# A gated mix of a state-space convolution and a bilinear GLU: first weights, four sums, ScalarE groups, last tile, dummy matmuls and plan numbers changed together

## The chip, the cores and the metric

The kernel runs on one core of a Trainium2 chip. The metric is the time of one execution on the device in microseconds (us), and lower is better. The core has a matrix engine (TensorE, PE in the profile, with its weight loads shown apart as PEld), VectorE (DVE), ScalarE (ACT), GpSimd (POOL) and SyncE (SP). Each engine takes its instructions in the order in which they were issued to it, and engines wait for one another by semaphores. Matmuls write to PSUM, of which the kernel uses eight banks of 128 partitions x 512 fp32 numbers (two for `y`, one each for `pg` and `pu`, four for everything else, `ps_k`). Transfers (DMAs) are issued from queues of SyncE, ScalarE and GpSimd.

## The reference

The input `x` has 2048 rows of 512 channels. Two branches work on it, and a gate for each row mixes them:

```python
x = A_u
g = _sigmoid((x * gate_w).sum(-1, keepdims=True))
a = _A_ref(x, ...)   # long convolution by FFT, with a kernel K made from 128 states per channel
b = _B_ref(x, B_w_gate, B_w_up, B_w_down)   # ((x Wg) * (x Wu)) Wd, with 1792 hidden columns
return g * a + (1 - g) * b
```

In branch a, `K = 2 Re sum_n C_n exp(A_n dt l)` for 2048 positions l and 512 channels; then `y = irfft(rfft(u) * rfft(K))` and `+ u * D_skip`. All numbers are fp32.

## The kernel before

**The GLU (branch b).** The 2048 rows are four tiles of 512 (`ci`), the 1792 hidden columns 14 blocks of 128 (`f`) in five groups (`GROUPS`). A hidden step, `hidden(f)`, multiplies a block of gate weights (`pg`) and of up weights (`pu`) with the tokens of a tile. There are 56 steps. Each fp32 operand is split into a high part, rounded to the matmul's own format, and the low rest (`split`: ScalarE copies the high part, VectorE subtracts), and three matmuls (`THREE`) replace one. The two products are multiplied into `h`, which is split into `hh` and `hl` by ScalarE and VectorE. `down` then multiplies the split `h` by the down weights into a sum `y` for each 128 rows (`r` = 0 to 3), over all blocks of the group. There are two PSUM banks for `y`.

**The sums.** `evacuate` scales a finished `y` by `ngate` = 1 - g of its rows (ScalarE, into one of three `acc` buffers) and stores it: the first time for a row tile by a plain store from SyncE, later by an accumulating transfer from GpSimd. The last tile of the last group goes another way, `ends`: what has been accumulated is read back into `sums` (in the profile `kt`), `product_in` adds the gated `y`, `transform_in` adds the convolution's last quarter, and `store` writes each 128 rows.

**The gate.** `u_part(c)` for c = 0 to 7 loads rows of `u`, makes the gate's scores with VectorE and the first transform with TensorE. After every second part, ScalarE and VectorE make `gate` and `ngate` for one tile of 512 rows.

**The convolution (branch a).** VectorE and ScalarE make tables of powers: `amplitudes` (21 exponentials for two blocks of channels, in three groups of seven), `phases` (sines) and the products. TensorE turns them into K and transforms K and u (`k_block`, `k_first`, `m_second`, `m_inverse`, `m_last`, all in the PSUM tag `k`). `finish` multiplies the result by the gate: eight ScalarE activations as one piece of work, except in the last quarter, where VectorE does it.

**The order of work.** Nothing runs in the order in which the code states it. Each `add(engine, us, fn, r=..., w=..., rank=...)` hands a piece of work to a planner (`Work`). The planner simulates all engines with the stated durations, takes the piece that can start first (ties by `rank`, lower first) and so writes out one fixed order for each engine. It knows buffer counts, a DMA rate (`DMA_RATE`), how far SyncE may issue ahead of the transfers (`AHEAD`), and the times at which TensorE's instruction code is fetched (`CODE...`; `recs` counts the instructions of a piece). Hidden step n may not be planned before `T_STEP * (n - 1)`. On the chip the engines keep the planned order but wait on semaphores, not on the planned times.

**The start.** `first_loads` loads tokens of tile 0 in four pieces (`x01`, `x23`; in the profile `y<-in_xT`) and the first two blocks of gate and up weights in eight pieces (`w01`; in the profile `ev<-in_wts`). Two of the eight go out on ScalarE's queue, both of block 1, and six on SyncE's. A piece is 128 partitions of two rows of 512 bytes. `split_block` splits a piece: ScalarE rounds (`whi`), VectorE subtracts (`wlo`). Meanwhile TensorE runs two dummy fp32 matmuls of 512 columns on a zeroed tile (`warm`); the profile shows each as two passes (`k<-acc`). `first_products` then takes blocks 0 and 1 together, in the order of the pieces.

Of the kernel before, what the change touches and what calls it, by code (L numbers as in the profile page):

```python
# [115 lines left out]
T_STEP = 10.1  # L116
# [30 lines left out]
class Work:  # L147
# [15 lines left out]
    CODE_US, CODE_BUS, PACE = 3.5, 0.9, 0.114  # L163
    DMA_RATE = 0.32
    AHEAD = 4.0
# [146 lines left out]
def gated_mix_kernel(  # L312
# [3 lines left out]
    xT: bass.AP,  # L316
    wts: bass.AP,
# [86 lines left out]
    def split(hi, lo, s, key):  # L404
# [9 lines left out]
        add("act", 0.62, lambda: act.copy(high(), src()), r=[got], w=[ph], rank=0)  # L414
# [19 lines left out]
    def first_loads():  # L434
# [9 lines left out]
        def first_w(f, kt):  # L444
            return w01.t[:, 2 * f : 2 * f + 2].rearrange("p c (k d) -> p c k d", k=KT)[:, :, kt]
# [159 lines left out]
    def down(y, r, h, w, first, last):  # L605
        def fn():
            for n, (a, b) in enumerate(THREE):
                pe.matmul(
                    y.t, h[a].t[:, r * P : (r + 1) * P], w[b].t, start=first and n == 0, stop=last and n == 2
                )  # L610

        add("pe", 0.684, fn, r=[*h, *w], w=[y], rank=2, recs=6)
# [3 lines left out]
    def evacuate(gi, ci, r, y):  # L616
# [4 lines left out]
        acc = new("glu", "acc", [P, D], bufs=3)  # L621
        add(
# [13 lines left out]
    def ends():  # L636
# [7 lines left out]
        def product_in(r, y):  # L644
            t = t0 + r
            add(
                "dve", 0.69,
                lambda: dve.scalar_tensor_tensor(
                    sums.t[:, r], y.t, ngate[:, t : t + 1], sums.t[:, r], op0=ALU.mult, op1=ALU.add
                ),  # L650
                r=[y, (m_gate, LAST)], w=[(sums, r)], rank=0,
# [12 lines left out]
        def store(r):  # L664
            add(
# [839 lines left out]
```

## Time and profile before

| what | us |
|---|---|
| median of 3 runs (602.71 to 603.29) | 602.87 |
| the profiled execution | 601.65 |
| its span, first to last instruction | 599.9 |
| ScalarE busy in it | 407.1 |
| sixteen matmul groups of K (`k<-v,x`) busy | 33.4 |
| matmuls of the GLU's last product (`y<-dhi,hl`), busy | 90.6 |

The profiled execution is one run of the program by itself, so its span and its time are compared with each other first and with the median afterwards. Rows of the views give the start (in order of time), the length, the engine, the operation and the tiles as output<-inputs; in brackets stands how long the engine had been idle before and what ended that. All rows name line L102, the helper that issues every instruction, so the tiles tell them apart.

### The profile page before, as it was taken

To read this page: it belongs to the slowest core of one execution; us is meant where nothing else is said; L and a number is where in the kernel's file an instruction comes from. 1 tells how busy PE (TensorE), PEld (TensorE's weight loads), DVE (VectorE), ACT (ScalarE), POOL (GpSimd) and SP (SyncE) were. 2 spreads that over 40 slices of the span, in tenths; PEclk is the share of its full clock that TensorE was granted. 3 is DMA by queue.
4 is the path that set the end of the run, shared out by engine and by line. 5 is a ranking of instruction groups with operands and counts; after the bars stand their busy time and mean duration, and the time that the engine had idled before them with its cause. 6 is when DMAs were issued, how large, how long until landed. Compare 5 with 4: busy or idle time off the path is not lost.

```text
span 599.9 us, 16215 instructions
## 1 busy us (share of the span) xinstructions
PE 590.1 (98%) x6628; PEld 452.7 (75%) x6628; DVE 513.7 (86%) x813; ACT 407.1 (68%) x923; POOL 106.4 (18%) x165
## 2 busy tenths in 40 slices
PE   8999999999999999999999999999999999999997
PEld 5667777777778877787877778787777777778875
DVE  6968999999999999999999998999999444874343
ACT  5658878875897887759789767869865545452330
POOL 0343443331212102010121101011110101211110
PEclk9999999999999999999999999999999999999999
DMA  8799968659859789399999849997994899997655
GB/s 264 221 343 343 317 211 285 205 147 277 210 121 291 206 238 320 65 306 211 301 228 254 224 125 274 215 302 156 309 233 156 209 212 297 253 239 164 158 83 112
DMA packets 102223, 136.22 MB, mean 227 GB/s; under 512 B 7300, under 2 KB 68228, under 8 KB 101124
## 3 DMA queue, kind: packets, MB, share of 16 engines
q1 hardware_dynamic: 80788, 100.57, 54.6%
q0 software_dynamic: 20672, 34.35, 28.6%
q8 instruction: 52, 0.85, 0.6%
q10 hardware_dynamic: 688, 0.26, 0.2%
q14 instruction: 23, 0.19, 0.1%
HBM read 77.75 MB, written 57.41 MB: 225 GB/s over the span
## 4 chain that ended last, share of the span: by engine, by line
PE 88%; DVE 7%; DMA 3%; issue 1%; ACT 1%; SPq 0%; DVEq 0%; POOLq 0%
PE pg L102 23%; PE pu L102 23%; PE y L102 22%; PE k L102 18%; DVE v L102 2%; DVE x L102 2%; DMA x_d<-x 1%; DMA s_d<-ts 1%; DMA ev<-in_wts 1%; DVE m L102 1%; DVE h L102 1%; DVE t L102 1%; DVE hl L102 1%; DVE ri L102 0%; DVE y L102 0%
## 5 line engine op out<-in xcount | busy, mean ns | idle before, releaser
L102 PE MATMUL pg<-x,whi 128*128 128x512 f32 x440 | 136.6, 390 | 0.8 <-ACT whi L102 0.8
L102 PE MATMUL pu<-x,whi 128*128 128x512 f32 x440 | 136.6, 390 | 0.0
L102 POOL DMA_DIRECT2D out<-acc x52 | 44.7, 924 | 304.9 <-ACT acc L102 293.7
L102 PEld LDWEIGHTS pg<-x,whi 128*128 128x128 f32 x440 | 82.6, 188 | 19.1 <-ACT whi L102 2.4
L102 PEld LDWEIGHTS pu<-x,whi 128*128 128x128 f32 x440 | 82.6, 188 | 16.9
L102 PE MATMUL y<-dhi,hl 128*128 128x512 f32 x224 | 90.6, 404 | 2.1 <-DVE hl L102 1.6
L102 PE MATMUL pg<-x,wlo 128*128 128x512 f32 x220 | 88.3, 402 | 0.1
L102 PE MATMUL pu<-x,wlo 128*128 128x512 f32 x220 | 88.0, 400 | 0.0
L102 PE MATMUL y<-dlo,hh 128*128 128x512 f32 x224 | 87.6, 391 | 0.0
L102 PE MATMUL y<-dhi,hh 128*128 128x512 f32 x224 | 87.3, 390 | 0.0
L102 ACT CAST hh<-h 128x512 fp32r<-128x512 f32 x56 | 34.8, 621 | 48.2 <-DVE h L102 47.6
L102 ACT ACTIVATE acc<-y,ngate 128x512 f32<-128x512 f32 x68 | 45.7, 687 | 27.2 <-PE y L102 18.4
L102 DVE TENSOR_TENSOR h<-pu,h 128x512 f32<-128x512 f32 x55 | 37.7, 685 | 27.6 <-PE pu L102 27.3
L102 PEld LDWEIGHTS y<-dhi,hl 128*128 128x128 f32 x224 | 42.0, 187 | 20.6 <-issue 4.8
L102 ACT COPY ts<-k 128x512 f32<-128x512 f32 (+1 forms) x112 | 47.7, 500 | 14.3 <-PE k L102 14.2
L102 PEld LDWEIGHTS pu<-x,wlo 128*128 128x128 f32 x220 | 41.3, 188 | 17.3 <-issue 8.2
L102 PEld LDWEIGHTS pg<-x,wlo 128*128 128x128 f32 x220 | 41.3, 188 | 15.5 <-issue 5.2
L102 PEld LDWEIGHTS y<-dhi,hh 128*128 128x128 f32 x224 | 42.1, 188 | 9.2
L102 PEld LDWEIGHTS y<-dlo,hh 128*128 128x128 f32 x224 | 42.1, 188 | 7.8
L102 ACT COPY h<-pg 128x512 f32<-128x512 f32 x55 | 32.2, 586 | 22.5 <-PE pg L102 14.5
L102 POOL DMA_DIRECT2D s_d<-ts x64 | 39.6, 626 | 40.7 <-ACT ts L102 36.3
L102 DVE TENSOR_TENSOR hl<-h,hh 128x512 fp32r<-128x512 f32 x56 | 38.4, 685 | 6.7 <-ACT hh L102 6.6
(117 smaller groups left out, 1006.3 us busy)
## 6 DMA issues: line engine op xcount, KB each, us to landing
x<-x_d SPq DMA_DIRECT2D x32, 512.0 KB, 6.2
out<-acc POOLq DMA_DIRECT2D x52, 256.0 KB, 6.7
in<-s_d SPq DMA_DIRECT2D x24, 512.0 KB, 6.0
raw<-in_wts SPq DMA_DIRECT2D x36, 256.0 KB, 4.6
x_d<-x POOLq DMA_DIRECT2D x16, 512.0 KB, 6.8
s_d<-ts POOLq DMA_DIRECT2D x64, 128.0 KB, 5.6
y_d<-ts SPq DMA_DIRECT2D x16, 512.0 KB, 5.6
raw<-in_xT SPq DMA_DIRECT2D x28, 256.0 KB, 5.0
```

What stands on the lines that cost most here:

```text
L102: got = getattr(self.engine, name)(*args, **kw)
```

## The change

- The first weights come from an input of their own, `in_w01`, laid out by the four row blocks `kt`: 128 partitions of 2 KB, of which block 0 is the first half. ScalarE's queue now loads `kt` = 0 for block 0 and then for block 1; SyncE loads both blocks of `kt` = 1 to 3 in one transfer each. The high part of the very first piece of tokens is copied by VectorE.
- The dummy matmuls are five of 256 columns.
- The sums of tile 0 in the first group are copied to `acc` first and gated there in place.
- The exponentials go in seven groups of three; the gating in `finish` goes in groups of two.
- In `ends`, `transform_in` goes ahead of `product_in`, and the last 128 rows are multiplied, added and stored in two halves of 256 columns.
- `T_STEP`, `CODE_US`, `CODE_BUS`, `DMA_RATE` and `AHEAD` have other values.

```diff
-T_STEP = 10.1
+T_STEP = 10.01
...
-    CODE_US, CODE_BUS, PACE = 3.5, 0.9, 0.114
-    DMA_RATE = 0.32
-    AHEAD = 4.0
+    CODE_US, CODE_BUS, PACE = 4.6, 1.0, 0.114
+    DMA_RATE = 0.327
+    AHEAD = 3.3
...
-        add("act", 0.62, lambda: act.copy(high(), src()), r=[got], w=[ph], rank=0)
+        if key == ("x", 0, 0):
+            add("dve", 0.4, lambda: dve.tensor_copy(high(), src()), r=[got], w=[ph], rank=0)
+        else:
+            add("act", 0.62, lambda: act.copy(high(), src()), r=[got], w=[ph], rank=0)
...
         def first_w(f, kt):
-            return w01.t[:, 2 * f : 2 * f + 2].rearrange("p c (k d) -> p c k d", k=KT)[:, :, kt]
+            return w01.t[:, kt].rearrange("p (f c d) -> p f c d", f=2, c=2)[:, f]
...
-        def first_block(f, kt, engine="sp"):
-            rows_w = wts[f][:, : 2 * D].rearrange("p (c k d) -> k p c d", c=2, k=KT)[kt]
-            queue = act if engine == "act" else sp
-            add(engine, 0.42, lambda: queue.dma_start(first_w(f, kt), rows_w), w=[(w01, (f, kt))], dma=128, rank=-1)
-
-        first_block(1, 0, "act")
-        first_block(1, 1, "act")
+        def first_block(kt, f=None):
+            fs = range(2) if f is None else [f]
+            queue = sp if f is None else act
+            cs = slice(2 * P * fs[0], 2 * P * fs[-1] + 2 * P)
+            add(
+                "sp" if f is None else "act", 0.42, lambda: queue.dma_start(w01.t[:, kt, cs], w01s[kt][:, cs]),
+                w=[(w01, (f, kt)) for f in fs], dma=128 * len(fs), rank=-1,
+            )
+
+        first_block(0, 0)
+        first_block(0, 1)
         for kt in range(KT):
             first_x(kt)
-            first_block(0, kt)
-            if kt > 1:
-                first_block(1, kt)
+            if kt:
+                first_block(kt)
...
-        add("dve", 0.2, lambda: dve.memset(zero.t, 0.0), w=[zero], rank=-1)
+        add("dve", 0.2, lambda: dve.memset(zero.t[:, :256], 0.0), w=[zero], rank=-1)
...
-            for _ in range(2):
-                pe.matmul(scratch.t, zero.t[:, :P], zero.t, start=True, stop=True)
-
-        add("pe", 3.4, warm, r=[zero], w=[scratch], rank=-1, recs=8)
+            for _ in range(5):
+                pe.matmul(scratch.t[:, :256], zero.t[:, :P], zero.t[:, :256], start=True, stop=True)
+
+        add("pe", 4.3, warm, r=[zero], w=[scratch], rank=-1, recs=20)
...
-    def down(y, r, h, w, first, last):
+    def down(y, r, h, w, first, last, half=None):
+        cs = slice(0, D) if half is None else slice(half * D // 2, half * D // 2 + D // 2)
...
         acc = new("glu", "acc", [P, D], bufs=3)
+        if gi == 0 and ci == 0:
+            add("act", 0.59, lambda y=y: act.copy(acc.t, y.t), r=[y], w=[acc], rank=0)
+            y = acc
         add(
             "act", 0.69, lambda: act.activation(acc.t, y.t, AF.Copy, scale=ngate[:, t : t + 1]),
...
-        def product_in(r, y):
+        def product_in(r, y, half=None):
             t = t0 + r
+            cs = slice(0, D) if half is None else slice(half * D // 2, half * D // 2 + D // 2)
             add(
-                "dve", 0.69,
+                "dve", 0.69 if half is None else 0.42,
...
+            add(
+                "sp", 0.42, lambda: sp.dma_start(ov[:, t, cs], sums.t[:, r, cs]), r=[(sums, (r, half))], w=[(m_out, (t, half))],
+                dma=256 if half is None else 128, rank=-1,
             )
...
         for r, y in ending[:2]:
+            transform_in(r)
             product_in(r, y)
-            transform_in(r)
-            store(r)
         for r, y in ending[2:]:
             transform_in(r)
-        for r, y in ending[2:]:
-            product_in(r, y)
-            store(r)
+        product_in(*ending[2])
+        for half in range(2):
+            product_in(*ending[3], half)
...
-                        if f not in late:
+                        if gi + 1 == len(GROUPS) and ci == LAST and r == 3 and f == fs[-1]:
+                            for half in range(2):
+                                down(ys[r], r, hs[f], wd[f], False, half == 1, half)
+                        elif f not in late:
...
-        for n in range(3):
-            ks = range(7 * n, 7 * n + 7)
-            add("act", 0.17 + 1.29 * (n == 0) + 7 * (0.09 + 0.0009 * TB * len(bs)), lambda ks=ks: exps(ks), r=[par], w=[(e, n)])
+        for n in range(7):
+            ks = range(3 * n, 3 * n + 3)
+            add("act", 0.1 + 1.29 * (n == 0) + 3 * (0.09 + 0.0009 * TB * len(bs)), lambda ks=ks: exps(ks), r=[par], w=[(e, n)])
...
-            add("act", 3.0, gated, r=ga, w=[fin])
+            for j in range(2 * n):
+                ts = range(2 * j, 2 * j + 2)
+                add("act", 0.7, lambda ts=ts, gated=gated: gated(ts), r=[*ga, (fin, 0), (fin, 1)], w=[(fin, ("g", j))])
```

More of the change, by code (lines that the diff above doesn't have):

```diff
@@ L316, in gated_mix_kernel @@
     xT: bass.AP,
+    w01s: bass.AP,
     wts: bass.AP,
@@ L608, in fn @@
                 pe.matmul(
-                    y.t, h[a].t[:, r * P : (r + 1) * P], w[b].t, start=first and n == 0, stop=last and n == 2
+                    y.t[:, cs], h[a].t[:, r * P : (r + 1) * P], w[b].t[:, cs], start=first and n == 0, stop=last and n == 2
                 )
-        add("pe", 0.684, fn, r=[*h, *w], w=[y], rank=2, recs=6)
+        add("pe", 0.684 if half is None else 0.37, fn, r=[*h, *w], w=[y if half is None else (y, half)], rank=2, recs=6)
     ending, stored = [], set()
@@ L643, in ends @@
         )
-        def product_in(r, y):
+        def product_in(r, y, half=None):
             t = t0 + r
+            cs = slice(0, D) if half is None else slice(half * D // 2, half * D // 2 + D // 2)
             add(
-                "dve", 0.69,
+                "dve", 0.69 if half is None else 0.42,
                 lambda: dve.scalar_tensor_tensor(
-                    sums.t[:, r], y.t, ngate[:, t : t + 1], sums.t[:, r], op0=ALU.mult, op1=ALU.add
+                    sums.t[:, r, cs], y.t[:, cs], ngate[:, t : t + 1], sums.t[:, r, cs], op0=ALU.mult, op1=ALU.add
                 ),
-                r=[y, (m_gate, LAST)], w=[(sums, r)], rank=0,
+                r=[y if half is None else (y, half), (m_gate, LAST), (sums, r)], w=[(sums, (r, half))], rank=0,
+            )
+            add(
+                "sp", 0.42, lambda: sp.dma_start(ov[:, t, cs], sums.t[:, r, cs]), r=[(sums, (r, half))], w=[(m_out, (t, half))],
+                dma=256 if half is None else 128, rank=-1,
             )
@@ L662, in transform_in @@
             )
-        def store(r):
-            add(
-                "sp", 0.42, lambda: sp.dma_start(ov[:, t0 + r, :], sums.t[:, r]), r=[(sums, r)], w=[(m_out, t0 + r)],
-                dma=256, rank=-1,
-            )
         for r, y in ending[:2]:
+            transform_in(r)
             product_in(r, y)
-            transform_in(r)
-            store(r)
         for r, y in ending[2:]:
             transform_in(r)
-        for r, y in ending[2:]:
-            product_in(r, y)
-            store(r)
+        product_in(*ending[2])
+        for half in range(2):
+            product_in(*ending[3], half)
     def glu():
@@ L1366, in finish, with gated @@
                 continue
-            def gated(t0=t0, flat=flat):
-                for t in range(4 * n):
+            def gated(ts, t0=t0, flat=flat):
+                for t in ts:
                     act.activation(flat()[:, t], flat()[:, t], AF.Copy, scale=gate[:, t0 + t : t0 + t + 1])
-            add("act", 3.0, gated, r=ga, w=[fin])
+            for j in range(2 * n):
+                ts = range(2 * j, 2 * j + 2)
+                add("act", 0.7, lambda ts=ts, gated=gated: gated(ts), r=[*ga, (fin, 0), (fin, 1)], w=[(fin, ("g", j))])
         cs = slice(P * q, P * q + P)
@@ L1475 @@
         "in_xT": host(u[rows.T.reshape(L)].T),
+        "in_w01": host(
+            np.stack([by_tile(i["B_w_gate"])[:2], by_tile(i["B_w_up"])[:2]], axis=1)
+            .reshape(2, 2, P, KT, P)
+            .transpose(3, 2, 0, 1, 4)
+            .reshape(KT, P, 4 * P)
+        ),
         "in_wts": host(
```

## The prediction, made before the changed kernel ran

> **What bounds the kernel now.** I read the page first, then the waits of TensorE, then the busy time by stages, and last the order of time at three places that the change touches.
>
> ```profile
> span 599.9 us, 16215 instructions
> PE 590.1 (98%) x6628; PEld 452.7 (75%) x6628; DVE 513.7 (86%) x813; ACT 407.1 (68%) x923; POOL 106.4 (18%) x165
> ```
>
> TensorE (PE) is busy for 590.1 of 599.9 us. The matmuls are the same before and after, except for some dummy ones and the last output tile. So the change can win only what TensorE does not use: 9.8 us in all. The waits of TensorE say where these lie:
>
> ```profile
> PE y L102 <- DVE hl L102: 1.6, 3, 0.7
> PE k L102 <- DVE acc L102: 1.5, 1, 1.5
> PE pg L102 <- ACT whi L102: 0.8, 1, 0.8
> PE k L102 <- DVE in L102: 0.6, 1, 0.6
> PE y L102 <- ACT acc L102: 0.4, 1, 0.4
> PE k L102 <- issue: 0.2, 1, 0.2
> PE k L102 <- DVE y L102: 0.2, 1, 0.2
> PE y L102 <- DVE kt L102: 0.2, 1, 0.2
> ```
>
> They add up to 5.5 us. The other 4.3 us are the end, after the last matmul (tail, below). By stages (the columns are length, then the busy time of PE, PEld, DVE, ACT and POOL, the granted clock, the DMA share and GB/s):
>
> ```profile
> 30.00:45.00 15.00, 13.74 (x67) 9.33 (x66) 10.05 (x20) 8.41 (x28) 7.16 (x12) 1.00 1.00 342
> 240.00:440.00 200.00, 200.00 (x2873) 154.39 (x2871) 196.89 (x287) 159.46 (x383) 24.07 (x25) 1.00 0.89 227
> ```
>
> From 30 to 45 us TensorE idles for 1.26 us, while the DMA engines are full. From 240 to 440 us it never idles, and the granted clock is 1.00: nothing is to be had there. VectorE (DVE) is nearly full there as well (196.89 of 200), which matters for a rival below.
>
> **The head.** The first real matmul needs three things: the end of the dummy matmuls, the first piece of tokens (tile `x`), and the first rounded piece of weights (`whi`).
>
> ```profile
> 0.73 0.98 ACTq L102 DMA_DIRECT2D ev<-in_wts  x2
> 0.92 0.48 DVE L102 MEMSET acc<- 128x512 f32 x1 [0.92 <-PEq L1494]
> 1.46 3.78 PE L102 MATMUL k<-acc 128*128 128x512 f32 x4 [1.46 <-DVE acc L102]
> 4.71 0.62 ACT L102 CAST x<-y 128x512 fp32r<-128x512 f32 x1 [1.16 <-DMA y<-in_xT]
> 5.57 1.02 ACT L102 CAST whi<-ev 128x256 fp32r<-128x256 f32 x3 [0.24 <-DMA ev<-in_wts]
> 6.03 0.50 PE L102 MATMUL pg<-x,whi 128*128 128x512 f32 x1 [0.79 <-ACT whi L102]
> ev<-in_wts ACTq DMA_DIRECT2D x2, 128.0 KB, 4.6
> L102 DVE TENSOR_SCALAR x<-v 128x512 f32<-128x512 f32 x1 | 0.4, 427 | 0.0
> ```
>
> Tokens are there at 4.71, and ScalarE (ACT) rounds them for 0.62 us. The weights that SyncE sent second are there only at 5.57. Rounding them brings the first matmul at 6.03, 0.46 us after their landing. After the change the block that is needed first leaves ScalarE's queue first, at 0.73; with the 4.6 us of that queue it lands at about 5.3 (estimate), and the first matmul could start at 5.3 + 0.46 = 5.8. The tokens no longer stand in its way: VectorE takes their high part, at the 0.43 us of the nearest one-source row, and is done by 4.71 + 0.43 = 5.14. The low part follows on VectorE's own queue, 0.2 us sooner than behind ScalarE's copy. The dummy matmuls: 4 passes over 512 columns took 3.78 us, 0.9 each, so 10 passes over 256 columns take about 4.3 to 4.7. The memset is half as wide (0.24 instead of 0.48), so they start at 1.22 and end at 5.5 to 5.9. They last about as long as the data takes. I take 5.7, a little under the 5.8 because the rows of the new block are twice as long: a gain of **0.3 us**. Three of SyncE's issues fall away (three double blocks instead of six), so its later loads only come sooner. Bounds: 0.7 (landing at 4.7 like the tokens, dummies sped up) and a loss of 0.1 (second block late; it is wanted two matmuls after the first).
>
> [...]
>
> **The four ungated sums.** These rows are TensorE's, ScalarE's and VectorE's in order of time:
>
> ```profile
> 30.77 0.39 PE L102 MATMUL y<-dhi,hh 128*128 128x512 f32 x1
> 34.07 1.09 PE L102 MATMUL k<-y,w_t 32*64 32x512 f32 x8 [0.19 <-DVE y L102]
> 34.56 0.21 ACT L102 ACTIVATE gate<-gate 128x4 f32<-128x4 f32 x1 [5.09 <-DVE y L102]
> 35.79 1.09 PE L102 MATMUL k<-in,w_t 32*64 32x512 f32 x8 [0.64 <-DVE in L102]
> 36.53 1.26 ACT L102 ACTIVATE acc<-y,ngate 128x512 f32<-128x512 f32 x2
> 37.26 0.50 PE L102 MATMUL y<-dhi,hl 128*128 128x512 f32 x1 [0.38 <-ACT acc L102]
> 38.01 0.62 ACT L102 CAST x<-raw 128x512 fp32r<-128x512 f32 x1 [0.23 <-DMA raw<-in_xT]
> 38.66 0.69 DVE L102 TENSOR_TENSOR x<-raw,x 128x512 fp32r<-128x512 f32 x1 [0.48 <-ACT x L102]
> 41.47 0.39 PE L102 MATMUL pg<-x,wlo 128*128 128x512 f32 x1
> L102 ACT COPY h<-pg 128x512 f32<-128x512 f32 x55 | 32.2, 586 | 22.5 <-PE pg L102 14.5 <-DVE hl L102 6.2 <-DVE ev L102 1.3
> ```
>
> The first two sums of tile 0 are complete at 31.2 (30.77 + 0.39); they fill both `y` banks and sit there until the gate exists, at 36.5. In the meantime TensorE has only the first transform of `u`, whose inputs VectorE is still making. It waits 0.19 + 0.64 + 0.38 = 1.21 us. With a plain copy (0.59, the nearest row of the same shape) ScalarE empties both banks by 31.2 + 2 x 0.59 = 32.4, in the 5.09 us in which it now waits for the gate, so the four copies (4 x 0.59 = 2.4 us) are covered: the first two wholly, the others where ScalarE has 6.6 of 15 us free (row 30 to 45). Then the 18 matmuls that now start at 37.26 (4.2 us to 41.47) can fill the hole. What is late next is the last quarter of the next tokens: rounded from 38.01, its low part is done by 38.66 + 0.69 = 39.35, and TensorE wants it at 41.47 - 1.21 - 0.3 = 39.96. That leaves 0.6 us. I take **1.0 us**, with bounds 0 (tokens as late as the gain) and 1.6 (the two halves of the transform also run without the drain between them). The fourth sum finds no free `acc` buffer (three, and the gate must come first) and keeps its bank as now.
>
> **ScalarE's groups in pieces.** The gated groups of eight now go in twos, and the exponentials in threes instead of sevens. No instruction is added; other work of ScalarE can now step in between.
>
> ```profile
> 2.26 1.28 ACT L102 ACT_TABLE_LOAD   x1 [2.26 <-issue]
> ```
>
> Every wait of TensorE is in the list above, and besides the gate's only the three for `hl` can hang on ScalarE, 1.6 us together. I take 0 of them, with bounds 0 and 1.6; the second rival has them all. If a sine steps in between two pieces of exponentials, ScalarE loads its tables twice more, 2.6 us. That costs TensorE nothing as long as it has other work, which it had throughout from 240 to 440 us; without that cover it is another wait for `hl`, and counted with the third rival.
>
> **The plan's numbers.** `T_STEP`, `CODE_US`, `CODE_BUS`, `DMA_RATE` and `AHEAD` only change the order in which the planner puts work, on every engine and queue. 0.09 us less per hidden step is 5 us at the last of 56. The code fetches they plan for show in one wait of TensorE, 0.2 us, that I count as gone: **0.2 us**. The rest I take as 0, between -1 and +1: these are the `hl` waits that can go or come.
>
> **The tail.**
>
> ```profile
> 595.00 0.19 PEld L102 LDWEIGHTS y<-dhi,hh 128*128 128x128 f32 x1
> 595.22 0.39 PE L102 MATMUL y<-dhi,hh 128*128 128x512 f32 x1
> 595.65 0.75 DVE L102 SCALAR_TENSOR_TENSOR kt<-y,ngate,kt 128x512 f32<-128x512 f32 x1 [1.29 <-PE y L102]
> 596.43 0.33 SPq L102 DMA_DIRECT2D out<-kt  x1
> L102 DVE SCALAR_TENSOR_TENSOR v<-v 128x256 f32<-128x256 f32 x16 | 6.7, 419 | 0.0
> DMA to landing us min/median/max: 2.0/2.0/2.3
> ```
>
> From the last matmul's end (595.61) to the span's end pass 4.3 us: VectorE 0.75, the store 2.3 from its issue, and 1.2 for the ending. Afterwards three matmuls become six of half width. The 18 matmuls above took 4.21 us, 0.234 each; half of it is 0.117, but each brings a weight load of 0.19. I take 0.19, between 0.117 and 0.234. The last of six starts at 594.76 + 5 x 0.19 = 595.71 and ends 0.27 later, at 595.98 instead of 595.61. VectorE starts 0.04 after it, as now, and needs 0.48: 0.75 less 0.27, the difference between 0.69 (512 columns, above) and 0.42 (256). The store leaves at 596.53, 0.10 later than now; the one of the first half has left SyncE's queue by then (0.33 each). It carries 128 KB instead of 256; at the 342 GB/s of the stage above that is 0.38 less. The sum is a gain of **0.25 us**: at best 0.5 (0.117 per matmul), at worst a loss of 0.3 (0.234, and a landing of 2.3 whatever the size).
>
> [...]
>
> The order of the last sums changes too. The transform's part (`kt<-kt,ts`) goes ahead of the first product:
>
> ```profile
> 585.56 0.49 DVE L102 TENSOR_TENSOR kt<-kt,ts 128x128 f32<-128x128 f32 x2
> 590.42 1.43 DVE L102 SCALAR_TENSOR_TENSOR kt<-y,ngate,kt 128x512 f32<-128x512 f32 x2 [1.26 <-PE y L102]
> ```
>
> The transform is done by 585.56 and the first product starts at 590.42, so a slip of more than 4 us would have to come first. It costs nothing, and two stores no longer wait for it.
>
> **Sum.** 0.3 + 1.0 + 0.2 + 0.25 = 1.75 us. The profiled execution took 601.65, 1.77 more than its span, and the median of the runs is 602.87, 1.22 above that. I take the gain off the median: 602.87 - 1.75 = **601.1 us**.
>
> **The rivals.**
> - *The hole is only moved.* If the tokens' last quarter is late by 0.6 us or more, or the fourth sum's held bank stops the next tile, TensorE waits there instead; the ungated sums then don't do what they are for. For it: the DMA engines are at 1.00 from 30 to 45 us. Against: the 0.6 us to spare. The gain left is 0.75: 602.1. Chance 0.23.
> - *The new plan also removes the waits for `hl`.* All 1.6 us of them: 601.1 - 1.6 = 599.5. For it: they are few and early, where the order changes most. Against: nothing in the change speaks of them. Chance 0.16.
> - *VectorE's queue makes hidden steps late, and the kernel gets slower.* `hl` and its product stand in VectorE's queue between table work, and VectorE is 98% busy from 240 to 440 us. With a shorter `T_STEP` the steps come earlier against the same table work. Three of 56 steps miss now, at 1.6 / 3 = 0.53 us each; six more cost 3.2 and outweigh the gain by 1.45: 604.3. It decides from the fourth added miss on (2.1 us over 1.75). Against it: TensorE does not idle from 240 to 440 for all that. Chance 0.11.
>
> **How the numbers follow.** The forecast has 0.50. A measurement of this kernel can tell about 0.2% from no change, 1.2 us. Faster by more: 0.46 of the forecast and the second rival, 0.62. Slower by more: the third, and 0.01 of the first, 0.12. Within: 0.26. The range leaves out the third rival, and the ends where all bounds fall on one side: 599.3 to 603.2.
>
> **What would show it.** Head: the first `pg` matmul at 5.5 to 5.9 instead of 6.03, and the dummies ending within 0.3 of it. Sums: no TensorE wait for `acc` or `in` between 30 and 40, four more ScalarE copies of 0.59. Tail: half-width matmuls 0.19 apart, and 3.7 us from the last matmul's end to the span's end. Plan: waits for `hl` stay near 1.6 us. The forecast is wrong if these rise above 3 us, or if a wait of TensorE for `x` stands where `acc` stood.

## The result, and the profile after

| | before | after |
|---|---|---|
| median of 20 runs each on one chip, us | 603.92 | 600.09 |
| profiled execution, us | 601.65 | 598.94 |
| its span, us | 599.9 | 597.2 |

The changed kernel takes 0.9944 of the time, with an interval from 0.9921 to 0.9968: about 3.4 us less. The forecast was 601.1 against 602.87, a ratio of 0.9971. So sign and range were right and the gain was about twice what I had said. Ratios and intervals leave out slow executions, those more than 1.5% above the fastest of their kernel: one of 972.81 us before, one of 2049.9 us after, and three of the six of the first kernel in experiment six. The two profiled executions differ by 2.7 us in span, and where these lie can be read from the traces.

The first lines of the page of the changed kernel (span, then busy time of each engine):

```profile
span 597.2 us, 16234 instructions
PE 589.5 (99%) x6637; PEld 454.0 (76%) x6637; DVE 511.6 (86%) x815; ACT 407.4 (68%) x926; POOL 106.3 (18%) x165
```

TensorE does the same work (589.5 against 590.1) in a span that is 2.7 shorter. Its waits, as shown of before:

```profile
PE k L102 <- DVE acc L102: 1.2, 1, 1.2
PE y L102 <- DVE hl L102: 1.0, 3, 0.4
PE pg L102 <- DVE x L102: 0.7, 1, 0.7
PE pg L102 <- ACT h L102: 0.3, 1, 0.3
PE y L102 <- DVE kt L102: 0.2, 1, 0.2
```

They sum to 3.4 instead of 5.5. The waits for `in`, for ScalarE's `acc`, for `y`, for `whi` and the one for "issue" are gone, and those for `hl` went from 1.6 to 1.0. (The `acc` that is left is the zeroed tile of the dummy matmuls.) Two are new, 0.7 for `x` and 0.3 for `h`. The two stages of before (length, then busy time of PE, PEld, DVE, ACT and POOL, granted clock, DMA share, GB/s):

```profile
30.00:45.00 15.00, 14.59 (x74) 10.54 (x73) 10.33 (x20) 10.84 (x33) 8.23 (x14) 1.00 1.01 359
240.00:440.00 200.00, 200.00 (x2646) 155.95 (x2645) 188.90 (x277) 154.11 (x374) 25.96 (x27) 1.00 0.87 221
```

From 30 to 45 us TensorE idles for 0.41 us instead of 1.26, and from 240 to 440 it still never idles. The hole itself, in order of time:

```profile
29.58 1.28 ACT L102 COPY acc<-y 128x512 f32<-128x512 f32 x2 [0.25 <-PE y L102]
...
30.75 0.39 PE L102 MATMUL y<-dhi,hl 128*128 128x512 f32 x1
...
35.41 1.95 ACT L102 ACTIVATE acc<-acc,ngate 128x512 f32<-128x512 f32 x3 [1.68 <-DVE ngate L102]
...
35.60 0.66 PE L102 MATMUL k<-y,w_t 32*64 32x512 f32 x4
35.63 0.66 PE L102 MATMUL k<-in,w_t 32*64 32x512 f32 x4
...
36.09 0.61 PE L102 MATMUL k<-y,w_t 32*64 32x512 f32 x4
36.11 0.61 PE L102 MATMUL k<-in,w_t 32*64 32x512 f32 x4
...
36.65 0.50 PE L102 MATMUL pu<-x,wlo 128*128 128x512 f32 x1
...
37.90 0.69 DVE L102 TENSOR_TENSOR x<-raw,x 128x512 fp32r<-128x512 f32 x1 [0.16 <-ACT x L102]
```

The two copies empty the banks from 29.58 on, the matmuls of the down product go on from 30.75, and the gating of the copies follows at 35.41 when `ngate` is there. The transform of `u` comes when both its inputs are done and takes 35.60 to 36.65, 1.05 us. Before it took 34.07 to 37.26, 3.19 us, and the two waits inside (0.64 and 0.38) are only 1.0 of the 2.1 that are gone. The rest is that the two halves now run side by side: the rows of `k<-in` start 0.03 after those of `k<-y` and lie over them, where before each half ran alone for 1.09 us. The kernel puts them on different column halves of the array (`tile_position=(32 * g, 64 * c)`). The kernel before did the same one part later, at 53.47:

```profile
53.47 0.66 PE L102 MATMUL k<-y,w_t 32*64 32x512 f32 x4
53.49 0.66 PE L102 MATMUL k<-in,w_t 32*64 32x512 f32 x4
```

Hidden step 4 starts at 40.4 instead of 43.0, and step 55, the last, at 578.8 instead of 581.4. So all 2.6 us are there by 41 us, and in sum nothing is added or lost in the 540 us that follow, although single steps between lie up to 10 us earlier (step 50 at 525.0 instead of 535.2).

The head of the changed kernel:

```profile
1.19 4.39 PE L102 MATMUL k<-acc 128*128 128x256 f32 x10 [1.19 <-DVE acc L102]
...
4.91 0.41 ACT L102 CAST whi<-ev 128x256 fp32r<-128x256 f32 x1 [1.49 <-DMA ev<-in_w]
...
5.34 0.42 DVE L102 TENSOR_TENSOR wlo<-ev,whi 128x256 fp32r<-128x256 f32 x1 [4.05 <-ACT whi L102]
5.69 0.42 DVE L102 CAST x<-y 128x512 fp32r<-128x512 f32 x1
...
6.07 0.41 ACT L102 CAST whi<-ev 128x256 fp32r<-128x256 f32 x1 [0.76 <-DMA ev<-in_w]
...
6.25 0.47 PE L102 MATMUL pg<-x,whi 128*128 128x512 f32 x1 [0.68 <-DVE x L102]
```

The dummies end at 5.58 and the first weights are rounded at 5.32, both a little earlier than I had taken. But on VectorE the low part of these weights stands ahead of the copy of the tokens, which therefore ends only at 6.11. The first matmul starts at 6.25, later than before (6.03). The tail:

```profile
592.25 0.28 PE L102 MATMUL y<-dhi,hl 128*128 128x256 f32 x1
592.25 0.19 PEld L102 LDWEIGHTS y<-dlo,hh 128*128 128x128 f32 x1
...
592.84 0.28 PE L102 MATMUL y<-dhi,hh 128*128 128x256 f32 x1
593.16 0.88 DVE L102 SCALAR_TENSOR_TENSOR kt<-y,ngate,kt 128x256 f32<-128x256 f32 x2 [1.33 <-PE y L102]
```

The six half-width matmuls start 0.118 apart ((592.84 - 592.25) / 5). The first half is complete after three of them, at 592.76, but in the trace only the last of the six releases VectorE, which starts on both halves at 593.16. From the last matmul's end (593.12) to the span's end pass 4.1 us, before 4.3.

### The profile page after: what moved, and what is told of

Read it like the earlier page. It is cut to its first block, busy times and chain, and to the rows that moved or that the text cites. A ratio compares the mean times of both kernels' runs of the same rounds, so it can differ in the third digit from the quotient of the medians.

```text
span 597.2 us, 16234 instructions
## 1 busy us (share of the span) xinstructions
PE 589.5 (99%) x6637; PEld 454.0 (76%) x6637; DVE 511.6 (86%) x815; ACT 407.4 (68%) x926; POOL 106.3 (18%) x165
## 4 chain that ended last, share of the span: by engine, by line
PE 77%; DVE 13%; issue 3%; ACT 3%; DMA 3%; POOL 0%; DVEq 0%; ACTq 0%; POOLq 0%
PE pu L102 20%; PE pg L102 20%; PE y L102 20%; PE k L102 17%; DVE x L102 4%; DVE v L102 2%; DMA out<-acc 2%; DVE m L102 1%; DVE y L102 1%; DVE hl L102 1%; ACT ts L102 1%; DMA x_d<-x 1%; DVE t L102 1%; DVE h L102 1%; DMA ev<-in_w 1%
## 5 line engine op out<-in xcount | busy, mean ns | idle before, releaser
L102 PEld LDWEIGHTS pu<-x,whi 128*128 128x128 f32 x440 | 82.6, 188 | 16.7
L102 PE MATMUL y<-dhi,hl 128*128 128x512 f32 (+1 forms) x225 | 91.3, 406 | 1.4 <-DVE hl L102 1.0
L102 PE MATMUL y<-dlo,hh 128*128 128x512 f32 (+1 forms) x225 | 87.8, 390 | 0.0
L102 PE MATMUL y<-dhi,hh 128*128 128x512 f32 (+1 forms) x225 | 87.5, 389 | 0.0
L102 ACT ACTIVATE acc<-y,ngate 128x512 f32<-128x512 f32 x64 | 43.5, 688 | 31.3 <-PE y L102 23.5
L102 PEld LDWEIGHTS pu<-x,wlo 128*128 128x128 f32 x220 | 41.3, 188 | 17.2 <-issue 7.8
L102 PEld LDWEIGHTS pg<-x,wlo 128*128 128x128 f32 x220 | 41.3, 188 | 15.6 <-issue 4.1
L102 POOL DMA_DIRECT2D s_d<-ts x64 | 39.7, 627 | 36.3 <-ACT ts L102 30.5
```

What stands on the lines that cost most here:

```text
L102: got = getattr(self.engine, name)(*args, **kw)
```

## The experiments

**The theory** after these traces: the four copies close the hole and give the whole gain; head and tail are small; the other parts give nothing at run time, but each of them changes the order that the planner writes out. **The rival** is the prediction's own book-keeping: each part has a price of its own, within 1 or 2 us, and the parts add up. They differ on what happens when one part is undone or done alone. All ratios are against the kernel before, measured alongside on the same chip.

**One: the four sums gated from the bank again.**

```diff
-        if gi == 0 and ci == 0:
-            add("act", 0.59, lambda y=y: act.copy(acc.t, y.t), r=[y], w=[acc], rank=0)
-            y = acc
```

> The changed kernel with the first tile's four sums gated straight from the bank again; all else stays. Theory (the ungated sums carry the gain): TensorE waits again between 31 and 43 us, hidden step 4 starts near 43 instead of 40.4, and the span is about 599.8, 2.6 above the changed kernel's 597.2. Rival (the new plan numbers carry it): step 4 may start late, but later steps catch up and the span stays within 1 us of 597.2. Second rival (the two early waits cost less than they show): span 598.2 to 598.6.

Measured: 636.64 us, ratio 1.0538 [1.0506, 1.0571]. Neither a gain of 1 us nor one of 3 is undone here but some 36. Its largest waits of TensorE:

```profile
PE k L102 <- DMA v<-y_d: 11.4, 2, 11.1
PE k L102 <- DVE y L102: 7.0, 3, 3.1
PE y L102 <- DVE kt L102: 5.9, 1, 5.9
```

The two rows of the old hole (0.64 for `in`, 0.37 for `acc`) are back at 34.86 and 36.32, and step 4 starts at 42.9, 2.5 later than in the changed kernel; a second hole of 3.05 stands at 56.42 where the next part of the transform waits for VectorE's `y`. The 2.5 are the worth of the copies. The second hole is already the work of another order, and most of the other 30 us come at the other end. The tile view of the convolution's last matmuls (ns shortest/median/longest, start of the first and the last), in this experiment:

```profile
L102 PE MATMUL k<-v,w_t x32: 623/1057/1059, 614.0 to 618.8; 64*32 64x512 f32 x32
```

and in the changed kernel:

```profile
L102 PE MATMUL k<-v,w_t x32: 589/589/613, 575.5 to 576.8; 64*32 64x512 f32 x32
```

The convolution ends 42 us later, although the GLU's last step starts at 575.7, 3.1 us *earlier* than in the changed kernel. The planner had put GLU work first; at the end only the convolution was left, and TensorE waited for its transfers (`v<-y_d`).

**Two: the kernel before, with nothing but the ungated sums.** The three lines above are added to the old kernel.

> The kernel before with one thing changed: the first tile's four sums are copied out of the bank first and gated later. Theory (the ungated sums carry the gain): hidden step 4 starts near 40.4 instead of 43.0, the waits of TensorE for the gate's sums and for the two halves of the transform are gone, and the span falls from 599.9 to about 597.3, with a ratio near 0.9955 to the kernel before. Rival (plan numbers): the span stays within 0.7 us of 599.9, since the old plan numbers put other work late. Second rival (half of it): 598.6.

Measured: 613.21, 1.0153 [1.012, 1.0185]: slower. Of its waits:

```profile
PE y L102 <- DVE hl L102: 3.2, 5, 1.3
PE pg L102 <- ACT h L102: 2.5, 3, 1.0
PE pg L102 <- ACT x L102: 1.1, 1, 1.1
```

No wait for `in` is left, but these have come in its place. The one for `x` is at 41.43, where TensorE waits for the tokens that ScalarE rounds: this is the first rival of the prediction, the hole that is only moved. Step 2 starts at 19.0 (17.2 in the kernel before) and step 4 at 44.3 (43.0): from the one to the other 25.2 us instead of 25.8, a gain of 0.6 where the changed kernel has 2.8. The late step 2 is not the copies' doing. The first matmuls of this execution are slow (last section), and that is 1.7 of the 12 us by which its span is longer. The convolution's last matmul starts only at 596.6.

**Three: the changed kernel with the five old numbers of the plan.**

```diff
-T_STEP = 10.01
+T_STEP = 10.1
...
-    CODE_US, CODE_BUS, PACE = 4.6, 1.0, 0.114
-    DMA_RATE = 0.327
-    AHEAD = 3.3
+    CODE_US, CODE_BUS, PACE = 3.5, 0.9, 0.114
+    DMA_RATE = 0.32
+    AHEAD = 4.0
```

> The changed kernel with the five old plan numbers (T_STEP, CODE_US, CODE_BUS, DMA_RATE, AHEAD). Theory (they only reorder): span 597.2 plus or minus 1, step 4 still at 40 to 41, waits for hl between 1 and 2 us. Rival (plan numbers carry the gain): span 599 to 600.5, with TensorE waits of 2 us or more after 45 us.

Measured: 618.17, 1.0237 [1.021, 1.0264]. Step 4 starts at 40.2, so the hole is closed and its gain is there. The numbers alone are worth some 18 us here. Its two largest waits both stand at the end:

```profile
PE k L102 <- issue: 8.1, 2, 7.4
PE y L102 <- DVE kt L102: 5.5, 1, 5.5
```

The 7.4 us end at 594.07, at the convolution's last matmuls; the GLU's last step had started at 574.7. The view calls this wait "issue", but the matmul there does wait for a semaphore, that of a transfer `v<-y_d` which was issued at 588.93 and landed at 593.98. So it is the wait of the first experiment again.

**Four: ScalarE's groups whole again**, three groups of seven exponentials and one of eight gatings.

```diff
-        for n in range(7):
-            ks = range(3 * n, 3 * n + 3)
+        for n in range(3):
+            ks = range(7 * n, 7 * n + 7)
...
-            for j in range(2 * n):
...
+            add("act", 3.0, gated, r=ga, w=[fin])
```

> The changed kernel with ScalarE's exponentials in three groups of seven and the gating of a quarter in one group of eight again. Theory 'each part sets the whole planned order': the order on every engine becomes another from early on, the convolution's last product ends later than the GLU's last step, and the time is 615 to 640, far more than the pieces themselves can cost. Rival, the prediction's own term (pieces are worth 0 to 1.6 us, the waits for hl): 599 to 602, hl waits 1 to 3 us.

Measured (two executions): 634.75, 1.0502 [1.0449, 1.0555], and the same picture as in the first experiment:

```profile
PE k L102 <- DMA v<-y_d: 12.2, 2, 11.8
...
PE y L102 <- DVE hl L102: 1.6, 3, 1.0
```

The waits for `hl`, the only ones that I had allowed this part, are 1.6, no more than in the kernel before. What the pieces alone do at run time can't be read from a run with another order, but what they do to the order is not small.

These four have one thing in common. The start of the convolution's last matmul (tile view) and the end of the span:

| kernel | last `k<-v,w_t` | GLU's step 55 | span | from the one to the end |
|---|---|---|---|---|
| before | 578.0 | 581.4 | 599.9 | 21.9 |
| after | 576.8 | 578.8 | 597.2 | 20.4 |
| sums gated | 618.8 | 575.7 | 635.8 | 17.0 |
| before, sums ungated | 596.6 | 585.7 | 612.0 | 15.4 |
| old numbers | 598.9 | 574.7 | 616.3 | 17.4 |
| whole groups | 615.5 | 568.9 | 633.0 | 17.5 |

In the two good kernels the convolution's last matmul comes before step 55, and the GLU's work covers what has to follow it. In the four others it comes 11 to 47 us after step 55, and 15 to 18 us follow it with little else to do.

**Five: only the two numbers for the landing of instruction code.** `CODE_US` and `CODE_BUS` go back to 3.5 and 0.9.

```diff
-    CODE_US, CODE_BUS, PACE = 4.6, 1.0, 0.114
+    CODE_US, CODE_BUS, PACE = 3.5, 0.9, 0.114
```

> The changed kernel with only CODE_US and CODE_BUS at their old values (3.5 and 0.9 instead of 4.6 and 1.0). The planner now believes that TensorE's instruction code lands 1.1 us sooner than with the new numbers. Theory 'the numbers have to fit the chip': in the blocks of many small matmuls (k<-v,x) TensorE runs out of instructions that the plan thought were there; its waits ended by 'issue' rise from nothing to 3 to 8 us, and the time to 602 to 608. Rival, the prediction's own term (these numbers are worth the one wait of 0.2 us): waits by 'issue' up to 0.5 us, time within 1 us of the changed kernel.

Measured: 605.2, 1.0004 [0.9971, 1.0038]. As a time, the whole gain is gone: the fastest of ten runs, 602.77, is slower than most of the changed kernel's, and the copy-first kernel of experiment seven, measured alongside, has 600.31. Its two largest waits:

```profile
PE k L102 <- issue: 2.1, 2, 2.0
PE pg L102 <- ACT h L102: 1.6, 2, 1.3
```

With the 1.3 more for `h`, the 2.1 for "issue" make up 3.4 of the 4.7 us by which this span (601.9) is longer than that of the changed kernel. But it is less than I had expected (2.1, not 3 to 8), and it is no proof of the theory. The long one stands at 165.85, in a group of matmuls which also stops for 2.3 to 2.6 us in three profiled executions with the new numbers (last section). So why the two numbers cost the gain stays open.

**Six: gated and ungated under other numbers.** Since an order can spoil a comparison, I took other numbers, meant to give an early end in all three forms: `T_STEP` 9.96, `CODE_US` 4.0, `CODE_BUS` 1.0, `DMA_RATE` 0.334 and `AHEAD` 3.5 for the changed kernel with the sums ungated and gated, and 10.0, 4.0, 1.0, 0.331 and 3.8 for the kernel before.

```diff
-T_STEP = 10.01
+T_STEP = 9.96
...
-    CODE_US, CODE_BUS, PACE = 4.6, 1.0, 0.114
-    DMA_RATE = 0.327
-    AHEAD = 3.3
+    CODE_US, CODE_BUS, PACE = 4.0, 1.0, 0.114
+    DMA_RATE = 0.334
+    AHEAD = 3.5
```

Ungated:

> The changed kernel with another set of plan numbers: T_STEP 9.96, CODE_US 4.0, CODE_BUS 1.0, DMA_RATE 0.334, AHEAD 3.5. Theory (the plan numbers matter only through when the convolution's chain ends): its last matmuls again start at least 15 us before TensorE's end, so the span is within 1 us of the changed kernel's 597.2. Rival (any other set of numbers throws the order): span above 605, with TensorE waiting for the chain at the end.

Gated:

> The same numbers as the run before, but the first tile's four sums gated straight from the bank. This is the pair that the run e1_gated failed to be, because there the convolution came last. Theory (ungated sums are worth the hole they fill, 1.7 to 2.6 us): step 4 starts 1.7 to 2.6 us later than in the run before, the convolution's last matmuls again lie 15 us before TensorE's end, and the span is 598.5 to 599.5. Rival (the sums carry all of what e1_gated lost): span above 605 again. Second rival (they carry nothing once the order is good): span within 0.7 of the run before.

The kernel before:

> The kernel before with another set of plan numbers and nothing else: T_STEP 10.0, CODE_US 4.0, CODE_BUS 1.0, DMA_RATE 0.331, AHEAD 3.8. Theory (plan numbers by themselves are worth 1 to 2 us of the gain): span 598 to 599.2 against 599.9. Rival (the gain needs the edits): span within 0.5 of 599.9. Third way (the order is thrown, as in e4_old_plan): above 605.

Measured: 616.53 (1.0131 [1.0082, 1.018]), 615.97 (1.0188 [1.0151, 1.0225]) and 608.13 (1.0079 [1.0049, 1.011]). As times these are misses; the first two can't be told apart, and all three are slower than the kernel before. Two things can be read from them. At step 4, before the orders have drifted, the pair stands at 39.7 and 42.5: 2.8 us for the copies, as in the first experiment (2.5). And the late end of the table above is not the only way to lose time. In all three the convolution's last matmul starts before step 55 (585.3 and 587.3, 593.9 and 596.0, 584.5 and 588.5). They lose it in waits all along, 8.5, 15.6 and 10.1 us in sum against 3.4 in the changed kernel, and in busy time (592.4 to 594.5 against 589.5). Among these waits are 3.14 for "issue" at 167.15 in the first and 4.4 in the second.

**Seven: the head, in three steps.** First VectorE's copy of the tokens ahead of the weights' low part, with the order on TensorE and ScalarE unchanged. `(xs[0], 0)` is the high part of the first tokens.

```diff
-            r=[(t, (f, kt)), (hi, ("b", kt))], w=[(lo, ("b", kt))], rank=0,
+            r=[(t, (f, kt)), (hi, ("b", kt)), *([(xs[0], 0)] if f == kt == 0 else [])], w=[(lo, ("b", kt))], rank=0,
```

> The changed kernel with one thing moved: VectorE copies the high part of the first tokens ahead of the first low part of the weights. The order on TensorE and ScalarE is the same. Theory: that place in VectorE's queue is what made the first matmul late (6.25 instead of 5.8); it now starts at 5.5 to 5.7. But the third and fourth matmuls belong to block 1, whose weights land only at about 6.0 and are rounded at 6.6, so TensorE waits 0.3 to 0.6 there and hidden step 2 starts at 17.2 to 17.4 as before: no difference in time (within 0.5). Rival (the copy's place alone cost the head's gain): step 2 at 16.8 to 16.9, time shorter by 0.4 to 0.6.

Measured: 600.31, 0.9949 [0.9922, 0.9975]. TensorE and ScalarE in order of time:

```profile
4.75 0.43 DVE L102 CAST x<-y 128x512 fp32r<-128x512 f32 x1 [3.46 <-DMA y<-in_xT]
...
5.40 0.85 PE L102 MATMUL pg<-x,whi 128*128 128x512 f32 x1
...
6.04 0.41 ACT L102 CAST whi<-ev 128x256 fp32r<-128x256 f32 x1 [0.69 <-DMA ev<-in_w]
...
6.50 1.11 PE L102 MATMUL k<-x,whi 128*128 128x512 f32 x2
```

The first matmul starts 0.85 us sooner than in the changed kernel (5.40), so the copy's place was what held it. The third, which needs the second block, starts only at 6.50, right after that block is rounded (6.45), and step 2 at 17.6, so nothing is won. But this execution says little of the second block, because its first matmuls are slow: 0.85 us for the first, 0.47 in the changed kernel. In the trace the granted clock is recorded as full only from 7.35 us, there from 5.19. The next run has it from 5.01.

Second, the same with block 0's matmuls of the first row block meant to go ahead of block 1's; the planner still put two of block 1 third and fourth.

> The changed kernel with the start mended: VectorE makes the high part of the first tokens before it subtracts the first weights (now the copy stands behind that subtraction and so behind ScalarE), and of the first row block TensorE takes all of weight block 0 before block 1, whose piece lands 1.2 us later. TensorE's order after the first twelve matmuls is untouched. Theory (the queue order on VectorE makes the first matmul late): the first real matmul at 5.5 to 5.6 instead of 6.25, no stall behind it, hidden step 2 at about 16.7 instead of 17.4, and the span 0.5 to 0.7 lower, about 596.6. Rival (the later token pieces or step 2's own inputs are the bound): the first matmul comes early, but step 2 still starts at 17.2 or later and the span does not move.

Measured: 599.96, 0.9937 [0.9914, 0.9959]; the first matmul at 5.55, the third at 6.66 after waiting 0.38 for `whi`, step 2 at 17.4. So the second block does hold TensorE once the copy does not. Third, with all six matmuls of block 0 really first:

```diff
-                for f, which in ((0, 0), (0, 1), (1, 0), (1, 1)):
+            runs = [(k, p) for f in range(2) for k in kinds for p in pairs if p[0] == f] if kt == 0 else slots
```

> The changed kernel with the start mended on both engines: VectorE copies the first tokens before it subtracts the first weights, and TensorE takes all six matmuls of weight block 0 in the first row block before those of block 1 (e7_first_block moved only two of them). Every other instruction keeps its place. Theory (block 1's late piece, wanted after two matmuls, is what holds the start): first real matmul at 5.6, no wait before 16 us, step 2 at about 16.7 instead of 17.4, step 4 about 0.6 earlier than 40.4, span about 596.6. Rival (the hole at 30 to 40 us is set by transfers, not by TensorE): step 2 early, but step 4 still at 40.2 to 40.6 and the span unmoved.

Measured: 599.5, 0.9951 [0.9928, 0.9974].

```profile
4.78 0.43 DVE L102 CAST x<-y 128x512 fp32r<-128x512 f32 x1 [3.49 <-DMA y<-in_xT]
...
5.43 0.49 PE L102 MATMUL pg<-x,whi 128*128 128x512 f32 x1
```

Now TensorE runs on from 5.43 and step 2 starts at 16.7, 0.7 sooner than in the changed kernel. At step 4 it is 0.3 (40.1): a wait of 0.51 for `hl` at 28.27, which the changed kernel does not have, has come in between. At step 8 it has become a loss of 0.5 (74.9 against 74.4), of which another, longer wait for `hl` is 0.3 (0.70 at 74.02, there 0.41 at 73.55). No version of the head is measurably better than the changed kernel.

**Eight: the last tile whole**, everything before it in the same order.

```diff
-        for half in range(2):
-            product_in(*ending[3], half)
+        product_in(*ending[3])
...
-                        if gi + 1 == len(GROUPS) and ci == LAST and r == 3 and f == fs[-1]:
+                        if False:
```

> The changed kernel with the last 128 rows multiplied, gated and stored whole again; the order of everything before is the same. In the changed kernel the six half-width matmuls start 0.12 apart, so they cost TensorE nothing; the gain is in VectorE's last piece (0.42 instead of about 0.7) and a landing 0.2 to 0.4 sooner. Expected from the last matmul's end to the span's end: 4.3 to 4.7 instead of 4.1, last matmul ending within 0.1 of 593.1 less the run's own shift, and the time longer by 0.2 to 0.6. Rival (the halves are worth nothing, because a store's length does not depend on its size): 4.1 to 4.3, and no difference.

Measured: 603.09, 0.997 [0.9942, 0.9998]. Its tail:

```profile
596.89 0.39 PE L102 MATMUL y<-dhi,hh 128*128 128x512 f32 x1
597.32 0.75 DVE L102 SCALAR_TENSOR_TENSOR kt<-y,ngate,kt 128x512 f32<-128x512 f32 x1 [1.29 <-PE y L102]
```

From the last matmul's end (597.28) to the span's end (601.8) pass 4.5 us, against 4.1 with the halves. But up to the landing of the last store it is 2.82 against 2.75. The other 0.4 comes after it, where 1.70 us pass until the span's end, and 1.31 in the changed kernel. In the first and third experiments, which have the halves, 1.7 us pass there too. So the halves are worth about 0.1, and not what the expectation gives them. The 3 us between the medians are something else: this execution has a wait of 2.5 us that the profiled one of the changed kernel does not have (last section). The ten runs fall in two groups, three from 598.87 to 599.93 and seven from 602.68 to 603.94.

## Why the prediction was right, and where it was not

- **What bounds the kernel: right in the main.** The gain lies before 45 us, and 240 to 440 us gave nothing. But "the change can win only what TensorE does not use" was too narrow: some 1.1 us came out of TensorE's busy time, where two groups of matmuls now overlap.
- **The head, 0.3 gained: wrong, 0.2 lost.** The step that failed is "is done by 4.71 + 0.43 = 5.14". I had taken it that VectorE makes the copy as soon as the tokens land. The copy stood behind the weights' low part in VectorE's queue, which itself waited for ScalarE, and was done at 6.11. The bound of a loss of 0.1 for the second block was right in kind: with the copy in front, that block stops TensorE (experiment seven). The landing (rounding starts at 4.91, I had 5.3) and the dummies (5.58, I had 5.7) were near. ScalarE's two weight transfers landed at 4.88 and 6.04, with the old rows at 5.10 and 5.97, so that the wider rows land sooner, on which I had put 0.1, no run shows. That the clock at the start differs from execution to execution had no term in the sum; in the last section step 2 starts at 19.0 instead of 17.2 with it, more than this whole term.
- **The four sums, 1.0: right in kind, too small, and outside its bounds of 0 to 1.6.** Step 4 comes 2.8 us sooner after step 2 (23.0 instead of 25.8). The step that failed is that I counted the waits in the transform's stretch (0.19 + 0.64 + 0.38), and for the upper bound a drain of 0.4 between its halves, an estimate that no run shows by itself, but not the stretch itself. The halves of the transform took 1.09 us each one after the other and now take 1.05 together. That is 2.1 less with the two waits between them, and the row at 53.47 of the kernel before could have told me. To this come the wait of 0.19 ahead of it and one of 0.56 for `hl` at 29.5 that is gone. Against it stand two that are left in the changed kernel: 0.30 for `h` at 40.38, and 0.11 at 38.65 for the low part of the tokens' last quarter, which I had named as next in line and which is itself 0.76 sooner (37.90 instead of 38.66). This makes 2.5; the other 0.3 shows in no wait. Two pairs of runs show about the same size, 2.5 and 2.8; in the old order the copies alone gave 0.6 (experiment two).
- **ScalarE's pieces, 0 of 1.6, and the plan's numbers, "The rest I take as 0, between -1 and +1": right for the whole, wrong as a price.** From step 4 to step 55 the two kernels gain and lose nothing against each other. But this holds only for all parts together. Undoing the five numbers costs 18 us (experiment three), two of them the whole gain (five), the pieces of ScalarE 35 (four). The sentence that the numbers "only change the order in which the planner puts work" was true, and the conclusion that this costs at most 1 us was not: an order that lets the GLU run ahead leaves the convolution alone at the end. That the whole came out at 0 is luck as far as the prediction goes, since nothing in its working could tell this set of numbers from those of experiments three, five and six. No sine stepped in between the pieces of the exponentials: both traces have 20 table loads of 1.28 us, one of them ahead of the first sine behind exponentials (`t<-t`, 49.81 before and 51.49 after) and one ahead of the first exponentials behind sines (`e<-pb`, 58.79 and 58.17).
- **The wait for "issue", 0.2 gained: gone in this execution, but not for good, and nothing is left of it at step 55.** See the last section.
- **The tail, 0.25: measured 0.2 against before, but put together otherwise.** The spacing of the half-width matmuls is 0.118, not the 0.19 that I took from the weight load's row; my lower end was 0.117. The weight loads are recorded at 0.19 each and yet follow one another 0.12 apart (592.25, 592.36, 592.48), so their recorded length did not set the spacing here. So the last matmul was as early as in my best case, and VectorE took that back: it makes both halves after the last matmul, 0.88 where I had 0.48 for one, since the first half starts only at 593.16. The last store landed 1.81 us after its issue and 2.29 before, a gain of 0.5 where I had 0.38. But with a whole tile in the same order it is 2.00 (experiment eight), so the size counts for only about 0.2 of it. With 0.15 lost after that landing (1.31 instead of 1.16) this makes 0.2. That it is near 0.25 is luck: the halves themselves are worth about 0.1.
- **The rivals.** The hole was not moved in the changed kernel (0.7 for `x` is the wait for the first tokens, at 6.25), but it was where the sums were ungated alone. The waits for `hl` fell by 0.6 of 1.6: the one at 29.5 went with the hole, and those after 45 us are 1.0 in both kernels. VectorE did not become the bound: 188.90 of 200 us from 240 to 440, less than before. The measured time is nearest to that of the second rival, for another reason. That it is only 1.0 from the forecast of 601.1 is partly luck: the kernel before, from which I took off the gain, has a median of 603.92 beside it, not the 602.87 of the three runs that I had.

So the sum was 0.3 + 1.0 + 0.2 + 0.25. By the marks of the profiled executions (step 2, step 4, step 55, the last matmul's end) it came out as -0.2 + 2.8 + 0 + 0.2, within 0.1 of the 2.7 by which the spans differ.

What stays open: why the planner's order becomes so much worse when one part is undone. The table shows that it lets the GLU ahead of the convolution; that this comes from taking whatever can start first, with small differences early that grow, is only argued. Open too is why the two numbers for the code cost the gain in experiment five, and what the new dummies are worth (last section).

## What to carry to other kernels

When a stage with waits moves, count its whole stretch and not the waits in it: matmuls that a wait drives apart may be ones that would have run side by side (here 1.09 us for each half, and 1.05 for both together). Where a planner writes the order, a part of a change has no price of its own: undo one part, and the order and the end may both become others. So compare early marks (here step 4) for what an edit does, and the end of each chain and the sum of the waits for what the order does. Before marks of two executions are compared, see that their first matmuls take equally long (here 0.40 in one and 0.63 in another). And before an operation is moved to another engine, ask what stands ahead of it in that engine's queue (here the first matmul started at 6.25 instead of 5.40).

## What the runs showed of the hardware that was not expected

**TensorE stopped inside a group of small matmuls, waiting for no semaphore, and not in every run.** The changed kernel and the experiment with the copy first have the same order on TensorE. The group of 128 small matmuls that starts at 163.85 in the changed kernel runs through:

```profile
163.85 2.07 PE L102 MATMUL k<-v,x 128*32 128x64 f32 x128
```

In the experiment it stops after 112 (start, length, and in brackets the wait and what ended it):

```profile
165.00 1.84 PE L102 MATMUL k<-v,x 128*32 128x64 f32 x112
169.13 0.46 PE L102 MATMUL k<-v,x 128*32 128x64 f32 x16 [2.28 <-issue]
```

With the last tile whole it stops at the same place for 2.52 us. At these stops no semaphore is waited for. The instruction queue on the page (q8) moves 16 KB at a time; in the changed kernel such a transfer starts at 162.12, ahead of the group, and in the two others at 166.89 and 168.60, inside it. Both times the matmuls go on about 1.4 us after the end of that transfer (0.88 and 0.92 long). The kernel with the first block meant to go first, also with the new numbers, stops at this place too, for 2.56 us, and the other stops in the traces of this case at which no semaphore is waited for (0.15 to 4.4 us) all end 1.2 to 1.6 us after the end of such a transfer. So it is most likely the code that was missing, though no trace shows what such a transfer holds. The profiled executions took 598.94 without this wait, and 602.20 and 603.57 with it. Of the 4.6 us between the spans with the last tile whole (601.8) and in two halves (597.2), 2.5 are this wait, 0.5 the tail, and 1.1 a longer wait for `h` (1.4 instead of 0.3). Why the transfer comes later against the group in some executions (1.9 and 2.1 after its start instead of 1.7 ahead) the traces don't show.

**After some waits the granted clock was 0.50 and TensorE was slower.** In the first experiment, by stages at its end (columns as above, the granted clock third from the right):

```profile
590.00:600.00 10.00, 5.88 (x207) 3.77 (x193) 8.68 (x11) 2.25 (x4) 0.00 (x0) 0.92 0.51 133
600.00:612.00 12.00, 2.19 (x64) 1.52 (x64) 2.49 (x4) 1.07 (x2) 0.00 (x0) 0.50 0.84 203
612.00:620.00 8.00, 5.11 (x32) 0.93 (x32) 1.20 (x2) 0.59 (x1) 0.00 (x0) 0.57 0.27 59
```

While it waits for `v<-y_d` the clock falls to 0.50, and the convolution's last 32 matmuls then take 1057 ns instead of 589 (the tile view above). Where the ungated sums were added alone, they come late as well (the last at 596.6), but TensorE did not idle from 586 us on: there the granted clock is 1.00 and they take 589 ns. So in the first experiment the wait at the end was paid twice, in idle time and in slower matmuls. Some much shorter waits had the same behind them. After the hole of 3.05 at 56.42 in the first experiment the granted clock is 0.50 from 56 to 62 us, and after the stop of 3.14 at 167.15 in experiment six from 168 to 172. A stop of 2.56 had the same effect in the second step of experiment seven; the stops of 2.28 and 2.52 above did not.

**At the start the clock differs from execution to execution.** The second matmul behind the dummies, in the kernel before and then in the same with the ungated sums added (experiment two):

```profile
6.36 0.40 PE L102 MATMUL pu<-x,whi 128*128 128x512 f32 x1
6.76 0.63 PE L102 MATMUL pu<-x,whi 128*128 128x512 f32 x1
```

In the second, matmuls take 0.63 instead of 0.39 until 9.7 us, and step 2 starts at 19.0 instead of 17.2; the kernel before with other numbers (experiment six) is as slow until 10.4 and has step 2 at 19.3. The traces record the full clock from 9.77 and 10.44 in these two, and from 5.15 in the profiled execution before. All three have the old dummy matmuls. In the eleven profiled executions with the new ones it is recorded from 7.35 us at the latest, and step 2 starts at 16.7 to 17.8. So the new dummies may save up to 2 us in some executions, which the two profiled ones compared above can't show. No run has them alone, so this is a guess from fourteen executions.
